# Splitting the load of wq so that its first sixteen rows go ahead of w1

## The chip, the cores and the metric

The kernel runs on one core of a Trainium2 chip. The core has engines that run their own instruction streams: PE (TensorE, matrix products), DVE (VectorE), ACT (ScalarE), POOL (GpSimd) and SP (SyncE, which here only issues transfers). Sixteen DMA engines move data between the chip's main memory (HBM) and the core's on-chip memory of 128 partitions. A transfer is issued by one instruction on SP's or ACT's queue, is cut into packets for the DMA engines, and adds 16 to a semaphore when all of it has landed. The metric is the device time in microseconds; lower is better.

## The reference

It is one decoding step (one new token, batch of two) of an attention block mixed with a small dense block by a learned gate:

```python
x = A_x                                              # 2 x 1 x 512, bfloat16
g = sigmoid((x * gate_w).sum(-1, keepdims=True))
q = (x @ wq)                                         # wq: 512 x 4096, 32 heads of 128
scores = einsum("bhqd,bhkd->bhqk", q, k_cache) * 128 ** -0.5    # 4096 positions
o = einsum("bhqk,bhkd->bhqd", softmax(scores), v_cache)
a = o.reshape(2, 1, 4096) @ wo                       # wo: 4096 x 512
b = relu(x @ w1) @ w2                                # w1: 512 x 1376, w2: 1376 x 512
out = g * a + (1 - g) * b
```

All inputs are bfloat16. The two caches hold 2 x 32 x 4096 x 128 values each, 67.1 MB apiece; wq and wo have 4.2 MB each, w1 and w2 1.4 MB each. Every byte is used once.

## The kernel before

Almost all of the kernel is the reading of 145 MB. The loads stand in one list on SP's queue, in the order in which they are to come: w1 (line 267), wq (268), ten loads of K (269 to 273), nine of V (274 to 282), wo in two parts (283, 284), and w2 in six (285 to 290). Each DMA has a semaphore on which its reader waits. SP issues a load as soon as the buffer it goes to is free, which a marker of the last reader tells it; the issued loads then wait in the DMA engines' queues. ACT's queue issues two small loads at the start, the rows of x (265) and of gate_w (266).

The buffers are five slots of 32 KB per partition (`kv`, line 115). wq goes to slot 3 as 128 rows of 32 KB, one per partition: partition p holds rows 4p to 4p+3 of the matrix (line 232). w1 goes to `kt`, the buffer of K's turned pieces, as 128 rows of 11,008 bytes (lines 141, 233). The first load of K is 4 MB into slot 4, the second 8 MB into slots 0 and 1. The third, 8 MB, goes to slots 2 and 3, over wq, and so waits for the end of the projection of q (`pe_qr1`, line 273).

At the start `gate` (from line 298) turns x and gate_w with PE, and DVE makes from them `xTw`, the operand of the projection, and the gate. `q_proj` (from 330) multiplies it with wq in 32 products, the first of which waits for wq's semaphore (line 336); DVE and ACT copy the result, PE turns it, and `q_put` places it among zeros. `ffn_h` (from 366) then multiplies x with w1, in 44 products, and DVE and POOL finish that hidden row. PE's program has these in the order projection, turns of q, products with w1, and then the scores.

K is worked on in 64 pieces. DVE turns a piece of 128 x 2048 32-bit words (`k_turn`, line 386) into one of three buffers; the first of these is w1's place, and so the first turn waits for the products with w1 (`pe_h`). PE multiplies the piece with q in `k_scores`. After all of K come the softmax (`softmax`), the spreading of the weights (`spread`), V in nine jobs (`v_unit`, `v_extract`), the two projections (`project`, `ffn_f`, `ffn_last`) and the output, sent in two rows by SP and ACT.

The list of the program is written by helper functions: `sp(...)`, `act(...)`, `pe(...)` and so on append an instruction to an engine's list with the markers (`waits`) and DMA semaphores (`dwaits`) that it waits for. `rearrange("(p t) n -> p (t n)", t=4)` makes the view with one row per partition.

Of the kernel before, what the change touches and what calls it, by code (L numbers as in the profile page):

```python
# [85 lines left out]
def bass_gated_mix__gqa_block_cached__dense_activation_relu__decode_kernel(  # L86
# [28 lines left out]
    kv = sb("kv", [128, 5, 16384], dt.bfloat16)  # L115
# [38 lines left out]
    def psf(p0, p1, c0, n):  # L154
        return PSF[p0:p1, c0:c0 + n]
# [19 lines left out]
    sem = {n: nc.alloc_semaphore("sem_" + n) for n in names}  # L175
# [12 lines left out]
    def adder(engine):  # L188
        def add(fn, waits=(), signal=None, dwaits=()):
            P.add(engine, fn, waits=[marker(w) for w in waits], signal=marker(signal) if signal else None, dwaits=dwaits)  # L190
        return add

    pool, dve, act, pe, sp = (adder(e) for e in ("pool", "dve", "act", "pe", "sp"))
# [38 lines left out]
    wq_in = A_wq.rearrange("(p t) n -> p (t n)", t=4)  # L232
# [31 lines left out]

    act(lambda e: e.dma_start(x_sb[0:2, :], A_x.rearrange("b s d -> (b s) d")).then_inc(sem["x"], 16))
    act(lambda e: e.dma_start(x_sb[2:3, :], gate_w.rearrange("(o d) -> o d", o=1)).then_inc(sem["gw"], 16))
    sp(lambda e: e.dma_start(w1, w1_in).then_inc(sem["w1"], 16))
    sp(lambda e: e.dma_start(kv[:, 3, :], wq_in).then_inc(sem["wq"], 16))
    for g, (u, halves) in enumerate(segments):
        dst = kv[:, 4, :] if len(halves) == 1 else region[:, place(g) // 2, :]  # L270
        src = unit_in(k_rows, u)[:, 16384 * halves[0]:16384 * (halves[-1] + 1)]
# [58 lines left out]
    def q_proj():  # L330
        for n in range(8):
            for t in range(4):
                pe(lambda e, n=n, t=t: e.matmul(  # L333
                    psf(32 * (n % 4), 32 * (n % 4) + 32, (QR_B + n // 4) * BANK, 512), lhsT=xTw[:, t, :],
                    rhs=wq_sb[:, t, n // 2, :, n % 2, :], start=(t == 0), stop=(t == 3), tile_position=(0, 32 * (n % 4))),
                   dwaits=([(sem["wq"], 16)] if n == 0 and t == 0 else []),
                   waits=(["dve_xTw"] if n == 0 and t == 0 else []),
                   signal=(f"pe_qr{n // 4}" if n % 4 == 3 and t == 3 else None))
        for half in range(2):
            row = psf(0, 128, (QR_B + half) * BANK, 512).rearrange("p (h e d two) -> p e h d two", h=4, e=2, two=2)  # L340
            for e2 in range(2):
                dst = qrow[:, half, 2 * e2:2 * e2 + 2, :].rearrange("p two (h d) -> p h d two", h=4)
                src = row[:, e2]
                if half:
                    act(lambda a, dst=dst, src=src: a.activation(out=dst, in_=src, func=ACT.Copy),
                        waits=[f"pe_qr{half}"], signal=f"qrow{half}{e2}")
                else:
                    dve(lambda v, dst=dst, src=src: v.tensor_copy(out=dst, in_=src), waits=[f"pe_qr{half}"], signal=f"qrow{half}{e2}")  # L348
        for half in range(2):
            for j in range(4):  # L350
                pe(lambda e, half=half, j=j: e.transpose(qT_ps[:, (4 * half + j) * 128:(4 * half + j + 1) * 128],
                                                         qrow[:, half, j, :], ident16[:, :]),
                   waits=([f"qrow{half}{e2}" for e2 in range(2)] if j == 0 else []),
                   signal=("pe_q" if half and j == 3 else None))
# [189 lines left out]
    gate()  # L544
    selectors()
    q_proj()
    q_put(0)
    q_put(1)
# [66 lines left out]
```

## Time and profile before

| | |
|---|---|
| time, median of 3 runs | 344.25 us (344.39, 344.25, 344.21) |
| span of the profiled execution | 342.9 us (its time is one of those of this kernel and is not listed by itself) |
| bytes moved | 145.61 MB, mean 425 GB/s |
| PE busy | 197.8 us (58%) |
| DVE busy | 178.5 us (52%) |
| ACT, POOL busy | 23.1 us (7%), 19.9 us (6%) |
| SP's DMA queue, share of 16 engines | 98.5% |
| w1 from issue to landing | 5.8 us |
| wq from issue to landing | 15.0 us |

The span runs from the first to the last instruction; the time of a run also holds what lies around it. Shares are of the span. Lines that begin with a name of an engine and a line number count a group of instructions; "SPq" and "ACTq" are the engines' instruction queues, where DMAs are issued. In the view of stretches the columns are: the stretch, its length, busy time of PE, PE's weight loads, DVE, ACT and POOL with their counts, the granted clock of PE, the share of the DMA engines and GB/s. Packets count in the stretch in which they start, so a share there can pass 1. The trace also keeps a record of each DMA packet: its queue, size, start and duration.

### The profile page before, as it was taken

What the parts mean: (1) busy time and instruction counts of PE and PEld (TensorE: products, weight loads), DVE (VectorE), ACT (ScalarE), POOL (GpSimd) and SP (SyncE); (2) the same over time, 40 slices, a digit from 0 to 9 for tenths busy, and PEclk for the clock granted to TensorE, in tenths of its full rate; (3) what the DMA queues carried; (4) which work ended last, traced back from release to release, by engine and by line L of the source; (5) the groups of instructions that cost most, each with busy time, mean ns of one, the idle gap of its engine ahead of it and who ended that gap; (6) DMA issues with size and microseconds to landing.
All of it is one profiled execution on the core that took longest, in us unless ns stands there. A gap on an engine that the chain in (4) does not pass through costs nothing.

```text
span 342.9 us, 2540 instructions
## 1 busy us (share of the span) xinstructions
PE 197.8 (58%) x1228; PEld 54.3 (16%) x972; DVE 178.5 (52%) x127; ACT 23.1 (7%) x71; POOL 19.9 (6%) x36
## 2 busy tenths in 40 slices
PE   0177329799969799699799337220706043150656
PEld 0141001111111111111111013100303011020231
DVE  2239059899789899698999562220100103020121
ACT  1040000000000000000000240000000000000000
POOL 8000000000000000000000040110100101000000
PEclk9999959989999999989999858755656756565787
DMA  8998989899998999999999999999999999998996
GB/s 348 428 489 369 482 375 482 382 474 413 438 489 367 429 443 466 392 459 390 475 420 436 461 390 420 445 466 413 443 413 445 428 428 443 413 468 382 440 401 239
DMA packets 4196, 145.61 MB, mean 425 GB/s; under 512 B 469, under 2 KB 986, under 8 KB 1242
## 3 DMA queue, kind: packets, MB, share of 16 engines
q1 hardware_dynamic: 4178, 145.46, 98.5%
q8 instruction: 8, 0.13, 0.2%
q14 instruction: 2, 0.02, 0.0%
q10 hardware_dynamic: 8, 0.00, 0.0%
HBM read 145.46 MB, written 0.00 MB: 424 GB/s over the span
## 4 chain that ended last, share of the span: by engine, by line
DMA 68%; DVE 15%; PE 13%; ACT 1%; issue 1%; POOL 0%; SPq 0%; DVEq 0%
DMA kv<-in_A_k_cache_dram 31%; DMA kv<-in_A_v_cache_dram 23%; DVE kt L386 13%; DMA kt<-in_B_w_dram 9%; PE PS L461 6%; DMA kv<-in_A_wq_dram 4%; PE PS L407 3%; PE PS L197 3%; ACT kt L428 1%; PE PS L333 1%; DVE mpad L413 1%; DVE kt L471 1%; POOL ptm L444 0%; DVE qbuf L467 0%; DVE kt L432 0%
## 5 line engine op out<-in xcount | busy, mean ns | idle before, releaser
L386 DVE STREAM_TRANSPOSE kt<-kv 128x2048 f32<-128x2048 f32 x64 | 141.2, 2274 | 22.4 <-DMA kv<-in_A_k_cache_dram 22.3
L407 PE MATMUL PS<-kt,qbuf 128*128 128x512 bf16 x256 | 105.7, 413 | 31.8 <-DVE kt L386 26.3
L197 PE MATMUL PS<-kt,qbuf 128*128 128x512 bf16 x256 | 105.1, 411 | 0.0
L461 PE MATMUL PS<-kv,ptm 128*32 128x512 bf16 x512 | 46.5, 541 | 79.0 <-DMA kv<-in_A_v_cache_dram 76.0
L467 DVE TENSOR_TENSOR qbuf<-PS,maskc 128x512 f32<-128x512 f32 x9 | 6.2, 692 | 109.0 <-PE PS L461 109.0
L407 PEld LDWEIGHTS PS<-kt,qbuf 128*128 128x128 bf16 x256 | 25.5, 100 | 139.9 <-DVE kt L386 72.7
L461 PEld LDWEIGHTS PS<-kv,ptm 128*32 128x32 bf16 x512 | 19.0, 129 | 105.1 <-issue 98.6
L444 POOL COPY ptm<-kt 32x512 bf16<-32x512 bf16 (+1 forms) x18 | 11.5, 638 | 268.7 <-DVE rsum L475 175.6
L360 ACT ACTIVATE qbuf<-PS 32x8 bf16<-32x8 bf16 x40 | 7.9, 196 | 134.2 <-PE PS L197 132.7
L448 ACT ACTIVATE ptm<-kt 32x512 bf16<-32x512 bf16 (+1 forms) x9 | 5.3, 603 | 100.1 <-PE PS L461 98.7
L471 DVE TENSOR_REDUCE kt<-qbuf 128x128 f32<-128x512 f32 x9 | 9.3, 1028 | 0.3
L428 ACT ACTIVATE kt<-PS,negm 128x512 bf16<-128x512 f32 x8 | 5.4, 696 | 30.4 <-DVE negm L424 30.4
L333 PE MATMUL PS<-kv,xTw 128*32 128x512 bf16 x32 | 3.6, 629 | 5.9 <-DMA kv<-in_A_wq_dram 5.9
L478 PE MATMUL PS<-rsum,sell 128*32 128x1 f32 x4 | 0.4, 196 | 10.1 <-DVE rsum L475 10.1
L432 DVE STREAM_TRANSPOSE kt<-kt 128x1024 bf16<-128x1024 bf16 x4 | 5.0, 1245 | 1.7 <-ACT kt L428 1.4
L348 DVE CAST qrow<-PS 128x256 bf16<-128x256 f32 x2 | 2.4, 1396 | 6.4 <-PE PS L333 6.4
L508 PE MATMUL PS<-kv,oW 128*2 128x512 bf16 x32 | 3.4, 590 | 1.4 <-DMA kv<-in_A_wo_dram 1.4
L300 PE MATMUL PS<-ident,x_sb 3*128 3x3 bf16 x4 | 0.3, 166 | 6.2 <-DMA x_sb<-in_gate_w_dram 6.2
L486 PE MATMUL PS<-kt,selx 128*32 128x128 f32 x18 | 3.4, 328 | 0.3 <-DVE kt L471 0.3
L303 DVE COPY xT<-PS 128x12 bf16<-128x12 bf16 x1 | 0.2, 169 | 6.5 <-PE PS L300 6.5
L230 POOL MEMSET ptm<- 128x4096 bf16 x1 | 3.5, 3501 | 0.0
L413 DVE TENSOR_REDUCE mpad<-PS 128x1 f32<-128x2048 f32 x1 | 2.3, 2290 | 2.1 <-PE PS L197 2.1
(64 smaller groups left out, 44.2 us busy)
## 6 DMA issues: line engine op xcount, KB each, us to landing
kv<-in_A_k_cache_dram SPq DMA_DIRECT2D x4, 4096.0 KB, 31.6
kv<-in_A_v_cache_dram SPq DMA_DIRECT2D x2, 4096.0 KB, 27.0
kv<-in_A_wq_dram SPq DMA_DIRECT2D x1, 4096.0 KB, 15.0
kv<-in_A_wo_dram SPq DMA_DIRECT2D x1, 3072.0 KB, 29.3
kt<-in_B_w_dram SPq DMA_DIRECT2D x1, 1376.0 KB, 5.8
kv<-in_A_wo_dram SPq DMA_DIRECT2D x1, 1024.0 KB, 31.3
kt<-in_B_w_dram SPq DMA_DIRECT2D x1, 768.0 KB, 31.9
kt<-in_B_w_dram SPq DMA_DIRECT2D x1, 320.0 KB, 32.3
```

The costliest lines, as they stand in the source:

```text
L197: return e.add_instruction(mybir.InstMatmult(start_tensor_calc=start, stop_tensor_calc=stop, tile_size=(128, 128), tile_position=(0, 0), l ...
L333: pe(lambda e, n=n, t=t: e.matmul(psf(32 * (n % 4), 32 * (n % 4) + 32, (QR_B + n // 4) * BANK, 512), lhsT=xTw[:, t, :], rhs=wq_sb[:, t, n ...
L360: act(lambda a, hq=hq: a.activation(out=qbuf[32 * hq:32 * hq + 32, g % 2, :, :, 32 + 32 * hq], in_=cols[32 * hq:32 * hq + 32, u4 // 2, 2 * ...
L386: dve(lambda v: v.transpose(out=dst, in_=pairs[:, h, 64 * rr:64 * rr + 64]), waits=([f"pe_sc_{i - NKT}"] if i >= NKT else ["pe_h"] if i == ...
L407: return e.matmul(args[0], lhsT=args[1], rhs=args[2], start=first, stop=last)
L413: dve(lambda v: v.tensor_reduce(out=mpad[:, 0:1], in_=psf(0, 128, 0, 2048), axis=AX.X, op=ALU.max), waits=["pe_sc_63", "c_mpad"], signal=" ...
L428: act(lambda a, bk=bk, e2=e2: a.activation(out=blocks[:, bk, :, 16 * e2:16 * e2 + 16], in_=psf(0, 128, bk * BANK, 512).rearrange("p (r n) ...
L444: pool(lambda e, args=args: e.tensor_copy(**args), waits=waits, signal=f"pt_{j}_{hq}")
L448: act(lambda e, args=args: e.activation(func=ACT.Copy, **args), waits=waits, signal=f"pt_{j}_{hq}")
L461: pe(lambda e, m=m, t=t: e.matmul(psf(32 * t, 32 * t + 32, V_B[j % 2] * BANK, 512), lhsT=ptm[:, j % 2, 4 * m:4 * m + 4, :, :], rhs=rows[:, ...
L467: dve(lambda e: e.tensor_tensor(out=Y.rearrange("p (c d) -> p c d", c=4), in0=psf(0, 128, V_B[u % 2] * BANK, 512).rearrange("p (c d) -> p ...
L471: dve(lambda e: e.tensor_reduce(out=X2[:, u, :], in_=Y.rearrange("p (c d) -> p d c", c=4), axis=AX.X, op=ALU.add), waits=[f"dve_y{u}"], si ...
```

## The change

The load of wq is split in two. The first part is issued ahead of w1: rows 0 to 15 of the view with one row per partition, to partitions 0 to 15, sixteen rows of 32,768 bytes (512 KB in all). Then comes w1, as before, and then the other 112 rows, to partitions 16 to 127. Both parts add to the same semaphore, and so the first product of the projection waits for 32 instead of 16. Nothing else is touched; the same bytes go to the same places.

```diff
     act(lambda e: e.dma_start(x_sb[0:2, :], A_x.rearrange("b s d -> (b s) d")).then_inc(sem["x"], 16))
     act(lambda e: e.dma_start(x_sb[2:3, :], gate_w.rearrange("(o d) -> o d", o=1)).then_inc(sem["gw"], 16))
+    sp(lambda e: e.dma_start(kv[0:16, 3, :], wq_in[0:16, :]).then_inc(sem["wq"], 16))
     sp(lambda e: e.dma_start(w1, w1_in).then_inc(sem["w1"], 16))
-    sp(lambda e: e.dma_start(kv[:, 3, :], wq_in).then_inc(sem["wq"], 16))
+    sp(lambda e: e.dma_start(kv[16:128, 3, :], wq_in[16:128, :]).then_inc(sem["wq"], 16))
...
-                   dwaits=([(sem["wq"], 16)] if n == 0 and t == 0 else []),
+                   dwaits=([(sem["wq"], 32)] if n == 0 and t == 0 else []),
```

## The prediction

> **What bounds the kernel now.** I read the page's head and slices first (which resource is full), then the queues and the chain that ended last, then the issues, and last the first 36 us by stretches and by order of time.
>
> ```profile
> span 342.9 us, 2540 instructions
> ...
> DMA  8998989899998999999999999999999999998996
> ...
> q1 hardware_dynamic: 4178, 145.46, 98.5%
> ...
> DMA 68%; DVE 15%; PE 13%; ACT 1%; issue 1%; POOL 0%; SPq 0%; DVEq 0%
> ...
> kv<-in_A_k_cache_dram SPq DMA_DIRECT2D x4, 4096.0 KB, 31.6
> ...
> kv<-in_A_wq_dram SPq DMA_DIRECT2D x1, 4096.0 KB, 15.0
> ...
> kt<-in_B_w_dram SPq DMA_DIRECT2D x1, 1376.0 KB, 5.8
> ```
>
> The reader is to see that SP's queue (q1) keeps the 16 DMA engines at work for 98.5% of the span and that DMA heads the chain. A 4 MB transfer on an idle queue would need about 10 us (below), yet the median 4 MB load of K lands 31.6 us after its issue: some 20 us of other transfers stand ahead of it. The DMA queue never runs dry, and time lost by an engine early is not won back later.
>
> ```profile
> 0.73 0.40 SPq L267 DMA_DIRECT2D kt<-in_B_w_dram  x1
> 1.19 0.42 SPq L268 DMA_DIRECT2D kv<-in_A_wq_dram  x1
> ...
> 16.21 3.64 PE L333 MATMUL PS<-kv,xTw 128*32 128x512 bf16 x32 [5.90 <-DMA kv<-in_A_wq_dram]
> ...
> 25.91 8.89 DVE L386 STREAM_TRANSPOSE kt<-kv 128x2048 f32<-128x2048 f32 x4
> ```
>
> In order of time: w1 is issued at 0.73, wq at 1.19, the projection of q starts at 16.21 when wq has landed, and the first turn of K at 25.91.
>
> ```profile
> 0.00:2.10 2.10, 0.00 (x0) 0.00 (x0) 0.00 (x0) 0.52 (x1) 1.33 (x9) 1.00 0.17 32
> 2.10:2.80 0.70, 0.00 (x0) 0.00 (x0) 0.00 (x0) 0.70 (x1) 0.70 (x1) 1.00 0.76 204
> 2.80:3.50 0.70, 0.00 (x0) 0.00 (x0) 0.00 (x0) 0.06 (x1) 0.70 (x1) 1.00 0.70 299
> ...
> 36.00:340.00 304.00, 181.09 (x1096) 47.28 (x852) 162.01 (x106) 17.07 (x57) 11.47 (x18) 0.80 1.00 429
> ```
>
> The last column is GB/s: 204 and 299 in the first stretches with data, 429 for the rest. This slow start is the only place where the change could win. The packet records of the trace size it: of the 16 engines, six begin w1 at 1.77 to 1.93 us and ten at 2.41 to 2.60, on average 0.43 us after the first; and w1's 128 packets of 11,008 B last 413 ns in the median but 464 in the mean, an excess of 51 x 8 = 0.41 us per engine. Together 0.84 us per engine, the slowest one 1.06. From 3.3 us on every engine is at 26.7 GB/s, and at 27.0 with 32 KB rows (1.213 us each).
>
> **The change, part by part.** The sum stands against the profiled execution: span 342.9 us, with about 1.3 us around it to the median of 344.25 (runs 344.21 to 344.39); no other time is listed for it. What moves the span moves the time one to one.
>
> (a) One more DMA on SP's queue. SP issues w1, the rest of wq and the first two loads of K one issue later, 0.46 us (0.73 to 1.19). Each engine meanwhile has a 32 KB row, 1.21 us: covered, 0. Without that cover it would be +0.46. Its completion is one more 4-byte packet per engine, 9 ns: +0.01. ACT's and POOL's queues issue the same as before, but the row of gate_w, landed at 6.03 us behind seven of w1's packets, may come one row later or more (+1.2 to +4.9). From its use at 6.17 the input of the projection, xTw, is done at 9.45, and the projection waits till 16.21: 6.8 us of cover, cost 0.
>
> (b) w1 lands later by the duration of the first transfer. It is used by PE at 22.82, after q's projection; it landed at 6.5. Cover 16 us, cost 0.
>
> (c) PE's wait is for both parts of wq. wq and w1 have the same bytes before K as now, so q's projection starts when the same bytes have come. Behind that wait on PE stand q's transposes, w1's products (to 25.40) and then K's scores; DVE's first turn waits for those products, and SP's third load of K for the projection. That load is issued at 19.93 with 12 MB in the queue, some 29 us of transfers from 16.2, so it keeps 25 us of cover. The first turn has only about 0.5 us, but K's first 4 MB shift by the same amount as wq.
>
> (d) The unknown: sixteen rows that go to sixteen neighbouring partitions, all at once. Every large transfer in this trace covers 128 partitions, eight rows per engine at 27.0 GB/s. It can't tell whether the limit belongs to the engine or to the place where it writes: with 128 partitions, sixteen places of eight partitions each would give the same rows. If it is the engine, the 16 rows take 1.21 us, as much as those bytes cost now: +0. If all 16 shared one place they would take 16 x 1.21 = 19.4: +18.2. The nearest row on the low side is x: two rows of 1,024 B to partitions 0 and 1 ran as two overlapping packets of 44 ns on two engines, done in 52 ns, where one such packet takes 46. No sharing is seen, but 1 KB could sit in a buffer. It speaks for sixteen engines and only weakly for sixteen free places. I take four engines to a place, the geometric middle of 1 and 16: 4 x 1.213 - 1.213 = +3.64.
>
> [...] By the x row alone it would be 0. No large transfer of this trace shows which holds.
>
> (e) The 112 rows. Seven rows per engine are 8.49 us against 9.70 now, which pays back the engine's own row of the first transfer (already counted in d). If places are shared, twelve of sixteen still owe all their eight rows, 9.70 us, one row more than the engines' seven. And an engine's seven consecutive rows no longer match one place, so two engines can meet. Ends: 0, and +2.43 (two rows). I take one row, +1.21.
>
> (f) The slow start: ten engines begin late and the first packets are slow. A long first row can cover late descriptors. Ends: 0 and -0.84. I take half, -0.42; nothing shows whether descriptors or the first reads of memory are slow.
>
> Sum: +0.01 + 3.64 + 1.21 - 0.42 = +4.44 us, 344.25 + 4.44 = 348.7. Ends of this case: 3.64 - 0.84 = +2.8 (347.0) and 3.64 + 2.43 = +6.1 (350.3). Nothing later takes it back: all later loads stand behind.
>
> **The rivals.** Free places, start unchanged or half mended (same). The engine is the limit, d and e are 0, the slow start is due to the first reads and stays, or half of it goes: 344.26 down to 343.84. [...] Against it: ten engines start 0.6 us behind six, which looks like descriptors arriving in turn.
>
> Free places, start mended (faster). Place: 1.77 to 3.3 us. With one descriptor per engine in the first transfer, all sixteen begin by about 1.8 us, and the 1.21 us rows run while w1's descriptors arrive. Price -0.84 +0.01: 343.4; with the slowest engine's 1.06, 343.2. It decides if sharing costs less than 0.15 us and over 0.69 of the 0.84 us comes back. For it: the late starts and the row of x, which was on its engine at 1.67 us. Against it: packets on all engines were slow until 3.2 us, including second packets on engines that started early, which a missing first descriptor does not explain.
>
> Worse sharing (slower by more). Eight rows to a place instead of four, +8.5 us (352.8), or the 112 rows dealt so that neighbours go to all engines at once, four sharing in each of seven rounds, 7 x 3.64 = +25.5 on top (374). For it: nothing but that the trace has no transfer of 112 rows. Should the 112 rows use fewer engines, 14 of eight rows, that would be +1.2.
>
> [...]
>
> **How the numbers follow.** About 0.2% (0.69 us) is what a measurement of this kernel can tell from no change. Chances: four to a place 0.56 (348.7); worse sharing or fewer engines 0.06; free places with the start mended 0.18 (343.4); free places with it not or half mended 0.20 (344.0). So slower 0.62, same 0.20, faster 0.18. I give sharing more than half because the one row against it moved a 32nd of the bytes that an engine moves here, and because all packets from 11 to 64 KB show the same rate whatever their size, as a fixed path does. The range takes in the sharing case to its upper end and the free cases to the mended start: 343.3 to 350.4; the likeliest case alone is 347.0 to 350.3.
>
> **What would show it.** Sharing: the 16 packets of wq's first rows last about 4.9 us each instead of 1.21, GB/s from 2 to 6 us stands near 110 instead of 200 to 430, w1 lands near 11.3 us (now 6.5), and the projection starts near 20.6 instead of 16.21. Step e: packets of the other 112 rows above 1.213 us, in pairs. Step f: the first starts within 0.1 us of each other. Free places: first packets near 1.2 us, w1 landed near 7.7 and the projection at 15.3 to 16.2. The forecast is wrong if the first rows take under 2 us; the carry to the end is wrong if the projection shifts and the end does not.

## The result, and the profile after

The changed kernel takes 353.75 us (median of 4 runs, 353.47 to 354.09) against 344.23 us (344.15 to 344.39): a ratio of 1.0274, with a 95% interval of 1.0262 to 1.0287. That is 9.5 us slower, where +4.4 us was forecast and 350.4 us was the upper end of the range. The profiled run's own time is 353.47 us, with a span of 352.2.

From the page of the changed kernel: head, slices, queues, chain and issues.

```profile
span 352.2 us, 2541 instructions
...
GB/s 179 320 261 473 456 380 469 447 383 480 402 434 462 376 466 454 395 448 454 383 474 432 426 432 395 463 439 424 432 447 432 426 439 439 424 426 402 435 405 227
...
q1 hardware_dynamic: 4194, 145.46, 98.5%
...
DMA 77%; PE 14%; DVE 8%; issue 0%; SPq 0%; DVEq 0%
...
kv<-in_A_wq_dram SPq DMA_DIRECT2D x1, 3584.0 KB, 24.0
...
kt<-in_B_w_dram SPq DMA_DIRECT2D x1, 1376.0 KB, 10.0
...
kv<-in_A_wq_dram SPq DMA_DIRECT2D x1, 512.0 KB, 6.7
```

The same line of the kernel before:

```profile
GB/s 348 428 489 369 482 375 482 382 474 413 438 489 367 429 443 466 392 459 390 475 420 436 461 390 420 445 466 413 443 413 445 428 428 443 413 468 382 440 401 239
```

The engines are busy 98.5% of the span as before, yet the first three slices move 179, 320 and 261 GB/s, where it was 348, 428 and 489; the later ones move about what they moved before. So here a busy DMA engine was not one at its rate: the same bytes sat longer in it. The 512 KB that go first need 6.7 us to land, and the other 112 rows 24.0 us from issue.

In order of time, the same kernel:

```profile
0.74 0.39 SPq L267 DMA_DIRECT2D kv<-in_A_wq_dram  x1
1.18 0.41 SPq L268 DMA_DIRECT2D kt<-in_B_w_dram  x1
...
25.67 3.64 PE L334 MATMUL PS<-kv,xTw 128*32 128x512 bf16 x32 [15.35 <-DMA kv<-in_A_wq_dram]
```

The projection of q starts at 25.67 us instead of 16.21: +9.46. The span is 9.23 us longer and the time 9.5 us. What happens after wq gives almost nothing back (0.23 us of the span).

By stretches, the changed kernel (last column GB/s):

```profile
2.00:6.00 4.00, 0.00 (x0) 0.00 (x0) 0.00 (x0) 0.88 (x1) 3.71 (x9) 1.00 0.57 77
6.00:10.00 4.00, 0.53 (x6) 0.47 (x6) 1.86 (x4) 0.00 (x0) 3.43 (x1) 1.00 1.16 423
10.00:24.00 14.00, 0.32 (x2) 0.23 (x2) 1.18 (x7) 0.17 (x1) 0.00 (x0) 1.00 0.96 253
26.00:36.00 10.00, 6.90 (x84) 4.37 (x76) 3.43 (x5) 4.01 (x10) 0.09 (x1) 1.00 0.99 426
```

The kernel before, in the stretch that ends when the projection of q starts:

```profile
3.50:16.20 12.70, 0.84 (x6) 0.70 (x6) 4.29 (x11) 0.17 (x1) 5.63 (x9) 1.00 1.05 450
```

There are two slow places. From 2 to 6 us the sixteen rows stand on the engines (their packets count where they start, most of them before 2.0, which is why the row shows only 77); the packet records have them from 1.75 to 5.96 us, 3.63 us in the mean instead of 1.21. From 10 to 24 us, the 112 rows run at 253 GB/s; their packets last 2.00 us in the mean, and not one of the 112 lasts under 1.45. In between, w1 runs at its usual rate, but for its first packets (1.35 us in the mean instead of 0.41).

### The profile page after: what moved, and what is told of

The parts are those of the page before. It is cut to its first block, busy times and chain, and to the rows that moved or that the text cites. A ratio compares the mean times of both kernels' runs of the same rounds, so it can differ in the third digit from the quotient of the medians.

```text
span 352.2 us, 2541 instructions
## 1 busy us (share of the span) xinstructions
PE 196.4 (56%) x1228; PEld 54.1 (15%) x972; DVE 177.3 (50%) x127; ACT 23.1 (7%) x71; POOL 20.0 (6%) x36
## 3 DMA queue, kind: packets, MB, share of 16 engines
q1 hardware_dynamic: 4194, 145.46, 98.5%
## 4 chain that ended last, share of the span: by engine, by line
DMA 77%; PE 14%; DVE 8%; issue 0%; SPq 0%; DVEq 0%
DMA kv<-in_A_v_cache_dram 31%; DMA kv<-in_A_k_cache_dram 30%; DMA kt<-in_B_w_dram 9%; DVE kt L387 7%; DMA kv<-in_A_wq_dram 7%; PE PS L462 4%; PE PS L408 4%; PE PS L197 4%; PE PS L334 1%; PE PS L517 0%; DVE kt L472 0%; DVE qbuf L468 0%; DVE out_sb L580 0%; SPq L268 0%; SPq L267 0%
## 5 line engine op out<-in xcount | busy, mean ns | idle before, releaser
L408 PE MATMUL PS<-kt,qbuf 128*128 128x512 bf16 x256 | 107.9, 421 | 29.2 <-DVE kt L387 25.3
L197 PE MATMUL PS<-kt,qbuf 128*128 128x512 bf16 x256 | 107.3, 419 | 0.0
L462 PE MATMUL PS<-kv,ptm 128*32 128x512 bf16 x512 | 44.1, 518 | 82.1 <-DMA kv<-in_A_v_cache_dram 80.9
L462 PEld LDWEIGHTS PS<-kv,ptm 128*32 128x32 bf16 x512 | 18.1, 124 | 106.6 <-issue 101.1
L334 PEld LDWEIGHTS PS<-kv,xTw 128*32 128x32 bf16 x32 | 1.3, 134 | 16.9 <-DMA kv<-in_A_wq_dram 15.4
L346 ACT ACTIVATE qrow<-PS 128x256 bf16<-128x256 f32 x2 | 2.4, 1462 | 18.9 <-PE PS L334 18.9
```

The source lines that it names most:

```text
L197: return e.add_instruction(mybir.InstMatmult(start_tensor_calc=start, stop_tensor_calc=stop, tile_size=(128, 128), tile_position=(0, 0), l ...
L334: pe(lambda e, n=n, t=t: e.matmul(psf(32 * (n % 4), 32 * (n % 4) + 32, (QR_B + n // 4) * BANK, 512), lhsT=xTw[:, t, :], rhs=wq_sb[:, t, n ...
L408: return e.matmul(args[0], lhsT=args[1], rhs=args[2], start=first, stop=last)
L462: pe(lambda e, m=m, t=t: e.matmul(psf(32 * t, 32 * t + 32, V_B[j % 2] * BANK, 512), lhsT=ptm[:, j % 2, 4 * m:4 * m + 4, :, :], rhs=rows[:, ...
```

## The experiments

Each kernel below is the kernel before with other loads of wq at its start; the diffs are against it. The waits of the projection are set to the number of loads on wq's semaphore. Where extra rows are loaded, they go to slot 2, which nobody reads until K's third load has overwritten it. Each time is compared with the kernel before on the same chip (344.22 to 344.38 us). Except for the last two, each of these kernels was run once; times of one and the same kernel differ by up to 0.6 us here.

**The sixteen rows alone.**

```diff
+    sp(lambda e: e.dma_start(kv[0:16, 2, :], wq_in[0:16, :]).then_inc(sem["wq"], 16))
     sp(lambda e: e.dma_start(w1, w1_in).then_inc(sem["w1"], 16))
     sp(lambda e: e.dma_start(kv[:, 3, :], wq_in).then_inc(sem["wq"], 16))
```

> The sixteen rows are loaded once more than needed (first transfer, source rows 0 to 15, partitions 0 to 15 of slot 2, which nobody reads), then w1, then all 128 rows of wq in one load: the first step of the change without the load of 112 rows. Theory P (neighbouring partitions share four write places): packets of the first transfer 2.9 to 4.9 us each, w1 landed near 10 us as in the changed kernel (6.5 before), wq's own packets 1.21 us, projection at 16.2 + 3.9 = 20.1 us, time near 348.2 us. Theory M (the memory is slow at reading one stretch of 512 KB): the same numbers. Theory C (the first 32 KB rows of any program are slow): the same. If the 112 rows play no part, and all of the change's 9.5 us comes from the first transfer: projection near 25.7 us, 353.7 us.

Measured: 348.68 us. Packets of the first load 3.35 to 4.16 us, mean 3.70; the first packets of w1 1.39 us in the mean instead of 0.41; w1 landed at 10.80, and then wq's 128 rows at 1.22 us each. By stretches and in order of time:

```profile
10.00:20.00 10.00, 0.31 (x2) 0.23 (x2) 1.18 (x7) 0.17 (x1) 0.00 (x0) 1.00 1.10 472
```

```profile
20.56 3.64 PE L334 MATMUL PS<-kv,xTw 128*32 128x512 bf16 x32 [10.25 <-DMA kv<-in_A_wq_dram]
```

With wq in one load the stretch from 10 to 20 us is back at full rate, and the projection starts at 20.56, which is 4.35 us late, 1.21 of that for the extra bytes. So the first transfer costs 3.14 us. The rest of the 9.46, namely 25.67 - 20.56 + 1.21 = 6.32 us, belongs to the load of 112 rows, if the two costs simply add up.

**Source or destination.** Two more kernels have the same extra load, with either side spread over every seventh row.

```diff
+    sp(lambda e: e.dma_start(kv[0:16, 2, :], wq_in[0:106:7, :]).then_inc(sem["wq"], 16))
```

> As the run with the extra sixteen rows, but source rows 0, 7, 14 to 105 go to partitions 0 to 15 of slot 2 (which nobody reads). Theory P: packets 2.9 to 4.9 us, projection near 20.1, time near 348.2, as with neighbouring source rows. Theory M: packets near 1.2 us, projection near 17.4, time near 345.5. Theory C: 20.1 and 348.2.

Measured: 348.50 us, packets of 3.10 to 4.20 us.

```profile
20.54 3.64 PE L334 MATMUL PS<-kv,xTw 128*32 128x512 bf16 x32 [10.22 <-DMA kv<-in_A_wq_dram]
```

With the destination crowded, where the rows come from makes no difference; theory M falls.

```diff
+    sp(lambda e: e.dma_start(kv[0:106:7, 2, :], wq_in[0:16, :]).then_inc(sem["wq"], 16))
```

> As the run with the extra sixteen rows, with the same source rows 0 to 15 but destination partitions 0, 7, 14 to 105 of slot 2 (which nobody reads). [...] Theories M and C: packets 2.9 to 4.9 us as with neighbouring partitions, projection near 20.1, time near 348.2.

Measured: 346.64 us, packets of 1.71 to 2.36 us.

```profile
18.64 3.46 PE L334 MATMUL PS<-kv,xTw 128*32 128x512 bf16 x32 [8.33 <-DMA kv<-in_A_wq_dram]
```

That is 2.43 us late: the bytes' 1.21 and 1.22 more, instead of 3.14 more. The destination decides, so it is theory P and not the start (C), though spreading the rows did not take away the last 1.22 us. No packet is at 1.21, but this says little about sharing: the mean is 1.98 us, and the first rows of a load to all 128 partitions last 1.91 (wq first, below). The load also begins later than the one to neighbouring partitions, at 2.12 us instead of 1.78, and SP takes 0.60 us to issue it instead of 0.39.

**The order undone, the split kept.**

```diff
     sp(lambda e: e.dma_start(w1, w1_in).then_inc(sem["w1"], 16))
-    sp(lambda e: e.dma_start(kv[:, 3, :], wq_in).then_inc(sem["wq"], 16))
+    sp(lambda e: e.dma_start(kv[0:16, 3, :], wq_in[0:16, :]).then_inc(sem["wq"], 16))
+    sp(lambda e: e.dma_start(kv[16:128, 3, :], wq_in[16:128, :]).then_inc(sem["wq"], 16))
```

> The split is kept and the order undone: w1, then rows 0 to 15, then the other 112 rows. Theory P: w1 lands at 6.5 us as before; the sixteen rows take 4.2 to 4.9 us and the 112 rows some 14 us as in the changed kernel, projection near 25 us, time near 353. If being first was the cause (theory C): projection near 16.2, time near 344.3. If only the rows of the first transfer are slow and the 112 are slow by what it left behind: projection near 20, time near 348.

Measured: 354.62 us, the sixteen rows 3.79 us in the mean, the 112 rows 2.17.

```profile
26.74 3.64 PE L334 MATMUL PS<-kv,xTw 128*32 128x512 bf16 x32 [16.43 <-DMA kv<-in_A_wq_dram]
```

Going ahead of w1 is no part of the loss, which is even 1.07 us larger at the projection without it; the split has all of it.

In the next run the two loads are swapped again, 112 rows first:

> w1, then the 112 rows, then the sixteen: the 112 rows without anything crowded ahead of them. If their cost is their own: packets of 2.0 us as in the changed kernel, 14 us for the seven, then 3.6 to 4.9 us for the sixteen rows, time near 354. If they were slow because the sixteen rows had put the engines out of step: packets near 1.4 us, 10 us for the seven, time near 350.

Measured: 354.38 us; the 112 rows take 1.99 us in the mean (1.52 to 2.38) and the sixteen after them 4.12. The 112 rows are slow by themselves.

**How rows are dealt.**

```diff
-    sp(lambda e: e.dma_start(kv[:, 3, :], wq_in).then_inc(sem["wq"], 16))
+    sp(lambda e: e.dma_start(kv[0:64, 3, :], wq_in[0:64, :]).then_inc(sem["wq"], 16))
+    sp(lambda e: e.dma_start(kv[64:128, 3, :], wq_in[64:128, :]).then_inc(sem["wq"], 16))
```

> w1 first as before, then wq in two loads of 64 rows, to partitions 0 to 63 and 64 to 127, four rows per engine. Theory P with rows dealt in runs (engine 0 the first four rows, engine 1 the next four): every engine shares its place with one other all the time, packets 2.4 us, wq 8 x 2.43 = 19.4 us, projection near 25.7 us, time near 353.7. Theory P with rows dealt in turn (row 0 to engine 0, row 1 to engine 1): sixteen neighbours at once in each round, four to a place, packets 4.2 to 4.9 us, projection near 40, time near 368. If only loads of a count that is not a power of two are slow (theory N): packets 1.21, projection 16.2, time 344.3.

Measured: 355.22 us, packets 2.52 us in the mean, projection at 27.41. By stretches:

```profile
6.00:26.00 20.00, 0.85 (x6) 0.71 (x6) 4.08 (x11) 0.17 (x1) 3.42 (x1) 1.00 0.99 208
```

Half the rate of 426, as with two engines to a place. This fits rows dealt in runs (2.43 us expected) and not in turn (4.2 to 4.9). The time is 1.5 us above what was expected: shared packets last 2.52 and not 2.43 us, which makes 0.7, and the semaphore is complete 0.9 us after the last packet's end instead of 0.35, which makes 0.5; the rest stays open. A power of two as the count didn't help (theory N falls).

**Is it only the engines that share?** Three runs. The first puts two small loads among wq's halves: A, fourteen rows to partitions nine apart, and B, sixteen rows to partitions seven apart. That B has pairs of rows with one place and A has none was the author's estimate; no run shows which partitions share one.

```diff
     sp(lambda e: e.dma_start(w1, w1_in).then_inc(sem["w1"], 16))
-    sp(lambda e: e.dma_start(kv[:, 3, :], wq_in).then_inc(sem["wq"], 16))
+    sp(lambda e: e.dma_start(kv[0:118:9, 2, 0:8192], wq_in[0:118:9, 0:8192]).then_inc(sem["wq"], 16))
+    sp(lambda e: e.dma_start(kv[:, 3, 0:8192], wq_in[:, 0:8192]).then_inc(sem["wq"], 16))
+    sp(lambda e: e.dma_start(kv[0:106:7, 2, 8192:16384], wq_in[0:106:7, 0:8192]).then_inc(sem["wq"], 16))
+    sp(lambda e: e.dma_start(kv[:, 3, 8192:16384], wq_in[:, 8192:16384]).then_inc(sem["wq"], 16))
```

> Two small extra loads of 16 KB rows (to slot 2, read by nobody) are put between w1, the first half of wq's columns and the second half, both of which go to all 128 partitions. [...] 16 KB alone takes 0.61 us. [...] Time with no sharing at all is 344.3 + 0.61 + 0.61 = 345.5; with B's pairs at 1.21, 346.1.

Measured: 346.66 us. The first of load A's packets last 0.61 to 0.62 us, but the packets behind them up to 0.93; A and the half of wq after it lose 0.29 us per engine against 0.61 us a packet. B and its half lose 0.65 us, about one whole packet on every engine, and between 11.45 and 12.2 us not one of the 16 packets that start lasts under 0.80. The time is 0.56 us above the 346.1 that was expected with pairs. B behaves as if all engines waited, at 0.80 to 1.09 us a packet, less than the 1.21 of two. But A was not free either, probably because its rows overlapped in time with neighbouring loads. So the two cases were made longer. Here too, that rows nine apart share no place and that some of the rows six apart do was the author's estimate; for rows six apart 354 was expected whether only the engines that share are slow or all sixteen:

```diff
     sp(lambda e: e.dma_start(w1, w1_in).then_inc(sem["w1"], 16))
+    for o in range(4):
+        sp(lambda e, o=o: e.dma_start(kv[o:o + 118:9, 2, :], wq_in[o:o + 118:9, :]).then_inc(sem["wq"], 16))
     sp(lambda e: e.dma_start(kv[:, 3, :], wq_in).then_inc(sem["wq"], 16))
```

> Between w1 and the whole wq stand four extra loads of fourteen 32 KB rows each (slot 2, read by nobody), to partitions o, o+9, o+18 to o+117, with o from 0 to 3. [...] If only sharing costs: the 56 packets take 1.21 us, projection at 16.2 + 4.85 = 21.0 us, time near 349.2. If an engine is slow wherever it doesn't write to its usual partitions: packets well over 1.21, time above 351.

```diff
     sp(lambda e: e.dma_start(w1, w1_in).then_inc(sem["w1"], 16))
+    for o in range(4):
+        sp(lambda e, o=o: e.dma_start(kv[o:o + 91:6, 2, :], wq_in[o:o + 91:6, :]).then_inc(sem["wq"], 16))
     sp(lambda e: e.dma_start(kv[:, 3, :], wq_in).then_inc(sem["wq"], 16))
```

> As the run with rows nine apart, but four loads of sixteen rows, to partitions o, o+6 to o+90. [...] If a crowded place holds up all engines: hardly any at 1.21, all near 1.7 to 2.4, as in the load of 112 rows. The time is near 354 by both (344.4 + 4 x 2.43), since the slowest engines set it.

The stretch from 5.5 to 9.3 us, rows nine apart:

```profile
5.50:9.30 3.80, 0.26 (x4) 0.20 (x4) 2.38 (x3) 0.00 (x0) 3.80 (x2) 1.00 0.97 397
```

The stretch from 7.0 to 14.5 us, rows six apart:

```profile
7.00:14.50 7.50, 0.59 (x2) 0.50 (x2) 3.79 (x10) 0.17 (x1) 2.42 (x1) 1.00 1.00 210
```

Rows nine apart: 350.92 us. The 28 packets of the first two loads last 1.21 to 1.34 us: these two loads, each to fourteen partitions nine apart, ran at the full rate. Later the expectation of 349.2 failed: two packets at 7.59 and 8.22 us last 2.18 and 2.06 us (by their time probably wq's first ones, on the two engines that a load of fourteen rows leaves out), and the fourth load slows to about 2.0 us. Two loads at work at once may share places again; that this is why was not tested further. Between the two lies a limit to what follows: thirteen of the fourteen packets of the third load, which ran beside those two, still last 1.21 to 1.25 us. If the two were slow by sharing, that did not hold up the other engines at once.

Rows six apart: 354.03 us. Of the 64 packets, none is under 1.66 us, and the 48 of the last three loads all lie between 2.34 and 2.57. No row of the four loads is spared. That crowded places held up all sixteen engines is the author's reading; no run shows which of these rows share a place. In these two runs the source rows are spaced like the destinations, so that source rows six apart are slow by themselves is not excluded; the source alone was varied only where the destination was crowded.

**Can the slow start be mended without crowding?**

```diff
-    sp(lambda e: e.dma_start(w1, w1_in).then_inc(sem["w1"], 16))
     sp(lambda e: e.dma_start(kv[:, 3, :], wq_in).then_inc(sem["wq"], 16))
+    sp(lambda e: e.dma_start(w1, w1_in).then_inc(sem["w1"], 16))
```

> wq whole (128 rows) ahead of w1: long first rows on every engine, each to its own place. If late descriptors cause the slow start, the first rows cover them and up to 0.84 us comes back: 343.4. If the first reads are slow by themselves, nothing: 344.2. The projection starts near 12.9 us, the products with w1 are still done before K's first turn; no cost seen there.

```diff
+    sp(lambda e: e.dma_start(kv[:, 3, 0:2048], wq_in[:, 0:2048]).then_inc(sem["wq"], 16))
     sp(lambda e: e.dma_start(w1, w1_in).then_inc(sem["w1"], 16))
-    sp(lambda e: e.dma_start(kv[:, 3, :], wq_in).then_inc(sem["wq"], 16))
+    sp(lambda e: e.dma_start(kv[:, 3, 2048:16384], wq_in[:, 2048:16384]).then_inc(sem["wq"], 16))
```

> The same 512 KB of wq's bytes first as in the change, but as 4 KB of each of the 128 rows; w1 follows, then the other 28 KB of each row. Theory P: all sixteen places are used evenly, so the 9.5 us are gone: 344.2 to 344.6 (some 0.1 us for 4 KB packets). If a small first part of wq ahead of w1 is what costs, whatever its partitions: near 348 to 353.

Measured, against 344.38 us before: wq first 344.51 us, ratio 1.0005 (0.9995 to 1.0014); columns first 344.38, ratio 1.0002 (0.9992 to 1.0011). Neither is told from no change. With wq first the sixteen first rows last 1.91 us in the mean instead of 1.21: the start was slow with long rows to all 128 partitions too. The second run is the change's own idea, 512 KB of wq ahead of w1, on all 128 partitions: its 9.5 us are gone.

## Why the prediction was wrong, by its own steps

**Right.** The bound and the carry: engines busy 98.5% before and after, and a loss of 9.46 us at the projection came out as 9.2 of span and 9.5 of time. Steps a to c cost nothing that shows: the gate's row came in time for PE at 7.42 (6.17 before), and xTw was done at 9.46 (9.45 before), long before 25.67. Steps d and f together were +3.64 - 0.42 = +3.22; the run with the sixteen rows alone has 3.14. That these agree so well is partly luck. Step f's half did not come back: with wq first nothing was won, and in the changed kernel the first packets began 0.45 us apart (1.75 to 2.20), not within 0.1. If f is nothing here too, d alone is 3.14 and not 3.64. Four engines to a place, the author's choice between 1 and 16, still comes nearest (3.14 / 1.213 + 1 = 3.6), and the runs that spread source (348.50 us) and destination (346.64) show that it is the destination. No run shows the places themselves. Shown are the times: the sixteen rows had landed at 7.42 us, 5.7 us after their first packet began, and the 64-row loads ran at 208 GB/s, half of 426.

**Wrong: step e, the 112 rows.** It read: "I take one row, +1.21", with ends 0 and +2.43. Measured: 6.32 us. From the packets: 7 x (2.00 - 1.21) = 5.5 us; and the semaphore is complete 0.90 us after the last packet's end (24.73 to 25.63), against 0.53 with the sixteen rows alone, so that 5.9 of the 6.32 are found. K's first row behind them still lasts 0.48 us longer. Dealing in runs was foreseen ("an engine's seven consecutive rows no longer match one place, so two engines can meet"), but the working let only the engines that meet pay, and charged a row or two. By its own argument one row was already the least that sharing costs (twelve places still owe eight rows), before any two engines meet; it was taken as the middle. Measured, all 112 packets were slow: the shortest lasts 1.45 us, the longest 2.38, as with rows six apart (none under 1.66). The step treated sixteen engines as independent. With two packets' time for every engine in each round, an estimate, seven rounds have an upper end of 7 x 1.21 = +8.5 us, and the measured 6.3 lies below that. The prediction named sharing by the 112 rows but not that every engine would be slow: the term was five times too small, and the range, which allowed 2.43 us for it, ended 3.4 us below the measured time.

**The x row.** It was set against sharing: two rows to neighbouring partitions, each in 44 ns. That it was weak because 1 KB may sit in a buffer fits what the runs show: w1's first packets behind the sixteen rows last 1.35 us instead of 0.41, and the last of the sixteen records ends at 5.96 us while their semaphore is complete only at 7.42 (0.35 us after the last record in the kernel before). So here the records ended 1.46 us before their load was complete, and part of its cost appeared on the packets behind it.

**The rivals.** Both cases of free places fell. The start mended, wholly or by half, is excluded by wq first, where long rows to all 128 partitions still began slowly (1.91 us) and the time stayed the same (344.51). On that start, six engines at 1.77 to 1.93 us and ten at 2.41 to 2.60 average 0.47 us after the first, not 0.43 as the prediction has it; nothing hangs on the difference. Eight rows to a place gave 352.8, near the measured time, but by another way: the sixteen packets would have lasted 9.7 us each, and they lasted 3.63. The worse dealing (neighbours to all engines in turn, +25.5) fell with the 64-row loads, whose packets last 2.52 us and not 4.2 to 4.9; fewer engines for 112 rows isn't what the traces show either, since the 112 packets come in seven rounds with sixteen under way at a time.

**Left open.** Which partitions share a place is not shown, and so neither is whether an engine without a shared place is held up, nor how much crowding it takes. Shown is that no packet of rows six apart lasts under 1.66 us and none of the 112 under 1.45, while thirteen of fourteen in the third load of rows nine apart stay at 1.21 to 1.25. That the source rows have no part in the 112 rows' cost was not tested by itself. What makes the first 1.5 us slow isn't known: it is neither the order of wq and w1 nor the length of the first rows.

## What to carry to other kernels

A load to some of the partitions wasn't a smaller load to all of them here: 16 neighbouring partitions (3.63 us a packet instead of 1.21), two halves of 64 (208 GB/s) and even 112 of 128 (253) all ran below the rate of 426 GB/s, on sixteen engines that looked fully busy. The first two loads of fourteen rows nine partitions apart did not (1.21 to 1.34 us a packet): it mattered which partitions were written at once. To send part of a matrix ahead, cut its columns and keep all 128 partitions; here that cost nothing, and won nothing (344.38 us in both). To see such a loss, read GB/s beside the busy share, and the time of one packet beside its size.

## What was not expected of the hardware

No packet was spared: rows six apart gave 2.34 to 2.57 us for each of the 48 packets of the last three loads, and the 112 rows gave 1.45 to 2.38, where 1.21 is the time of a row in a load to all 128 partitions. That a few crowded places hold up all sixteen engines would explain it, but it was not shown. And the end of a packet's record was not the end of its load's cost: the records of the sixteen rows ended at 5.96 us, their semaphore was complete at 7.42, and w1's first packets behind them took 1.35 us, three times the usual 0.41.
